# The last two pairs of chunks' up-projection as one block product with seven products for eight

## The chip, the cores and the metric

One core of one Trainium2 chip. The metric is the device time of one execution in microseconds (us); the time before is 1064.84 us, the median of 3 runs.

## The reference

Banded causal attention, then a feed-forward layer on its output, all in 32-bit floats:

```python
scores = scale * q @ k.T          # 8 batches, 8 heads, 576 positions, head size 64
scores += slopes[h] * -abs(rel)   # kept where 0 <= rel < 128, else -1e9
attn = exp(scores - max) / (sum + 1e-9)
x = (attn @ v)                    # to 4608 tokens x 512
h = x @ w_in                      # 512 -> 2048
g = h * sigmoid(1.702 * h)
out = g @ w_out                   # 2048 -> 512
```

## The kernel before

The feed-forward part takes 18 chunks of T = 256 tokens in 16 steps each, one step per block f of 128 hidden columns. So that products keep nearly full precision, each factor is split into a high and a low part and three products are made: high by high, high by low, low by high. In a step `Job.up` (L547 to L563) makes 12 matmuls of 256 columns into one of two banks h_ps (4 blocks of 128 of the model width, three products), ACT makes the tanh (L557), DVE finishes the gelu (L558), ACT rounds it to its high part gh (L561), POOL subtracts to get the low part gl (L562). `Job.down` (L565 to L573) makes 6 matmuls of 512 columns into acc0 and acc1. The loop emits the next step's up ahead of this step's down, so that the gelu of one step lies beside PE's work on others. At a chunk's end `finish` evacuates both accumulators by DVE and sends them out from ACT's queue; at its start `split_x` splits the chunk's x.

Attention runs beside it in ticks. A unit is a pair of heads and up to two query blocks; a tick moves several units one stage on each: load, split, scores (PE), bias and minimum (DVE), exponent (ACT), normalisation (DVE), transposes (PE), high and low part of the probabilities (ACT, DVE), mix (PE), sum into the chunk's x (`sum_up`, ACT, POOL, DVE). Batches 2 to 7 have 20 units each. A batch may start once the chunk named in `due` has begun, and must be done three steps ahead of the chunk that first needs it; the loop spreads its ticks evenly over the steps between. For batch 7 these are the start of chunk 13 and the start of chunk 15.

The weights come as 64-bit words in the first part and are decoded by ACT, DVE and POOL into w1[f] and w2[f], each with a high and a low part, 512 KB of room each, kept to the end.

The order on each engine is not that of the source alone: a scheduler with a timeline of its own places the instructions (the source order is its priority), except those that `keep_in_program_order` pins, the loads among them.

Of the kernel before, what the change touches and what calls it, by code (L numbers as in the profile page):

```python
# [142 lines left out]
def tile_kernel(ctx: ExitStack, tc: tile.TileContext, q0, k0, v0, qT, kT, v, w_in, w_out, out):  # L143
# [388 lines left out]
    def split_x(c, x):  # L532
        xh = xp.tile([P, NC, T], F32R, name="xh")
        xl = xp.tile([P, NC, T], F32R, name="xl")
        for k in range(NC):
            (nc.scalar.copy if c in BESIDE else nc.vector.tensor_copy)(xh[:, k], x[:, k])
# [1 line left out]
            sub.tensor_tensor(xl[:, k], x[:, k], xh[:, k].bitcast(F32), ALU.subtract)
        return xh, xl

    class Job:

# [4 lines left out]

        def up(self, f):
            h = ps.tile([P, T], F32, name="h_ps", bufs=2)
            ops = [(z, x, k) for z, x in ((0, self.xh), (1, self.xh), (0, self.xl)) for k in range(NC)]  # L550
            for n, (z, x, k) in enumerate(ops):
                nc.tensor.matmul(  # L552
                    h, w1[f][:, z, k * P:(k + 1) * P], x[:, k],
                    start=(n == 0), stop=(n == len(ops) - 1))
# [132 lines left out]
    begin(jobs[0])
    seen = 0
    flat = [(j, f) for j in jobs for f in range(j.f0, j.f1)]
    for now, (j, f) in enumerate(flat):  # L690
# [10 lines left out]
        pace, last = 0.0, 0  # L701
        for n, by, start in due:
            if start > seen:
                break
            last = n + 3
            pace = max(pace, (n + 3 - ticks - credit) / max(starts[by] - 1 - SLACK - now, 1))
        credit += pace
        while credit >= 1 and ticks < last:
            credit -= 1
            tick()  # L710
# [63 lines left out]
```

## Time and profile before

| | |
|---|---|
| time, median of 3 runs (lowest, highest) | 1064.84 us (1064.75, 1067.0) |
| the profiled execution: its time, its span | 1068.36 us, 1066.3 us |
| mean granted clock of TensorE | 0.995 |
| matmuls | 7041 |
| DMA | 78.45 MB, mean 74 GB/s |

In the page PE is TensorE's matmuls, PEld its weight loads, which overlap them, DVE VectorE, ACT ScalarE, POOL GpSimd, SP the engine from which the loads are issued. A name ending in q is an engine's sequencer or queue. A matmul's recorded duration includes its pipeline; the pace of a stream is read from the chain in order of time, where each piece counts once. A row of the chain has its start, its length, and what ran; a row of the timeline has start, length, engine, line, operation, and in brackets how long the engine had been idle and who released it. Rows of groups have the count, busy time, mean ns of one, and the idle time ahead of them.

### The profile page before, as it was taken

The numbers are of one execution on the slowest core, as the hardware profiler recorded it, in microseconds if no ns is written. First come the engines' busy times: TensorE is split into PE (matmuls) and PEld (weight loads), VectorE is DVE, ScalarE is ACT, GpSimd is POOL, SyncE is SP. The second block draws the span as 40 slices with busy tenths as digits, with TensorE's granted clock in tenths as the row PEclk, the third lists the DMA queues.
The fourth block names the chain that finished last, engine by engine and source line by source line (L and its number), as shares of the span: only waits on it lengthen the run. The fifth ranks groups of instructions, "written<-read, shape, count | busy, mean of one in ns | idle before, by whom it ended". The sixth has DMA issues, their size and how long they took to land.

```text
span 1066.3 us, 21362 instructions
## 1 busy us (share of the span) xinstructions
PE 1052.9 (99%) x7041; PEld 929.1 (87%) x7041; DVE 660.5 (62%) x2117; ACT 597.2 (56%) x1811; POOL 603.5 (57%) x863
## 2 busy tenths in 40 slices
PE   9899999999999999999999999999999999999998
PEld 5567787889989999999999999999999999998987
DVE  6797522568887777545767668767877687313121
ACT  6879853466666565535555556655665656322222
POOL 4579933567676666554656557656666665323232
PEclk9899999999999999999999999999999999999999
DMA  8872001223222132102121223212222221000000
GB/s 307 281 261 73 25 22 56 73 67 96 75 76 81 51 102 67 57 14 71 54 79 52 71 62 91 66 60 78 79 63 85 57 78 28 20 2 20 1 21 20
DMA packets 88109, 78.45 MB, mean 74 GB/s; under 512 B 36800, under 2 KB 79296, under 8 KB 88000
## 3 DMA queue, kind: packets, MB, share of 16 engines
q1 hardware_dynamic: 82240, 67.14, 21.4%
q10 hardware_dynamic: 5760, 9.96, 2.6%
q8 instruction: 55, 0.90, 0.3%
q14 instruction: 54, 0.44, 0.1%
HBM read 67.63 MB, written 9.44 MB: 72 GB/s over the span
## 4 chain that ended last, share of the span: by engine, by line
PE 94%; DVE 3%; ACT 1%; DMA 1%; issue 1%; POOL 0%; SPq 0%; DVEq 0%; POOLq 0%; ACTq 0%
PE h_ps L552 38%; PE acc L571 37%; PE s_ps L334 5%; PE x_ps L499 5%; PE t_ps L442 4%; PE x_ps L476 2%; PE t_ps L419 1%; PE sb_ps L324 1%; PE s_ps L324 1%; DVE wc L213 1%; DMA rw<-w_out 1%; ACT pb L374 1%; DVE rec L392 0%; PE acc L189 0%; DVE rw L212 0%
## 5 line engine op out<-in xcount | busy, mean ns | idle before, releaser
L562 POOL TENSOR_TENSOR gl<-g,gh 128x256 fp32r<-128x256 f32 x288 | 218.0, 757 | 292.2 <-ACT gh L561 224.9
L552 PE MATMUL h_ps<-xh,w 128*128 128x256 f32 x2304 | 370.2, 284 | 1.1 <-POOL w L217 0.6
L552 PEld LDWEIGHTS h_ps<-xh,w 128*128 128x128 f32 x2304 | 328.5, 189 | 34.5 <-issue 2.8
L571 PE MATMUL acc<-w,gh 128*128 128x512 f32 x1152 | 324.9, 400 | 0.0
L558 DVE SCALAR_TENSOR_TENSOR g<-g,h_ps 128x256 f32<-128x256 f32 x288 | 119.6, 415 | 207.9 <-ACT g L557 206.5
L557 ACT ACTIVATE g<-h_ps 128x256 f32<-128x256 f32 x288 | 110.4, 383 | 229.4 <-PE h_ps L552 207.3
L571 PEld LDWEIGHTS acc<-w,gh 128*128 128x128 f32 x1152 | 196.5, 189 | 27.9 <-ACT g L557 0.3
L552 PE MATMUL h_ps<-xl,w 128*128 128x256 f32 x1152 | 194.6, 280 | 0.0
L561 ACT CAST gh<-g 128x256 fp32r<-128x256 f32 x288 | 116.9, 406 | 129.5 <-DVE g L558 121.1
L571 PE MATMUL acc<-w,gl 128*128 128x512 f32 x576 | 188.0, 401 | 0.0
L552 PEld LDWEIGHTS h_ps<-xl,w 128*128 128x128 f32 x1152 | 164.2, 188 | 6.0
L312 POOL TENSOR_TENSOR K<-rk,K 128x384 fp32r<-128x384 f32 (+1 forms) x120 | 109.0, 909 | 65.2 <-ACT Q L292 15.9
L381 ACT ACTIVATE pb<-pb,mins 128x256 f32<-128x256 f32 (+2 forms) x216 | 104.9, 487 | 43.8 <-DVE mins L362 40.1
L571 PEld LDWEIGHTS acc<-w,gl 128*128 128x128 f32 x576 | 92.6, 188 | 9.5 <-issue 0.9
L311 POOL TENSOR_TENSOR Q<-rq,Q 64x256 fp32r<-64x256 f32 (+1 forms) x120 | 83.1, 692 | 22.2 <-DVE K L310 4.9
L406 DVE TENSOR_SCALAR pb<-pb,rec 128x256 f32<-128x256 f32 (+2 forms) x216 | 91.8, 461 | 3.2
L362 DVE CUSTOM_DVE_ANT_0 pb<-s_ps,bias 128x256 f32<-128x256 f32 (+3 forms) x240 | 85.7, 377 | 4.1 <-PE s_ps L334 2.8
L392 DVE TENSOR_SCALAR rec<-sums 128x2 f32<-128x2 f32 (+3 forms) x144 | 48.5, 336 | 58.4 <-ACT pb L381 53.6
L334 PE MATMUL s_ps<-K,Q 128*128 128x256 f32 (+1 forms) x432 | 79.8, 289 | 0.4 <-DVE mins L362 0.4
L310 DVE CAST K<-rk 128x384 fp32r<-128x384 f32 (+1 forms) x120 | 52.5, 438 | 41.2 <-PE s_ps L334 34.2
L461 DVE TENSOR_TENSOR pl<-t_ps,ph 128x512 fp32r<-128x512 f32 (+2 forms) x120 | 72.2, 604 | 9.3 <-ACT ph L455 6.6
L442 PE MATMUL t_ps<-ident,pb 128*128 128x128 f32 x408 | 74.2, 272 | 0.0
(68 smaller groups left out, 1322.2 us busy)
## 6 DMA issues: line engine op xcount, KB each, us to landing
rk<-kT SPq DMA_DIRECT2D x72, 192.0 KB, 2.5
rq<-qT SPq DMA_DIRECT2D x96, 128.0 KB, 2.3
out<-o ACTq DMA_DIRECT2D x36, 256.0 KB, 2.1
rw<-w_in SPq DMA_DIRECT2D x16, 512.0 KB, 6.5
rw<-w_out SPq DMA_DIRECT2D x16, 512.0 KB, 7.0
rk<-kT SPq DMA_DIRECT2D x48, 128.0 KB, 2.2
rv<-v SPq DMA_DIRECT2D x96, 64.0 KB, 1.9
rq<-q SPq DMA_DIRECT2D x16, 128.0 KB, 2.6
```

Source lines behind the costliest of these rows:

```text
L312: nc.gpsimd.tensor_tensor(K2, rk, K1.bitcast(F32), ALU.subtract)
L334: nc.tensor.matmul(u.s[:b.rows, e, b.first:b.end], u.Q[:, b.q0 - u.q0:b.q0 - u.q0 + b.rows], k[:, ko:ko + b.end - b.first], start=(z == 0) ...
L362: nc.vector.tensor_tensor_reduce(b.p[ra:rb, cs:b.end], u.s[ra:rb, e, cs:b.end], bias[head][ra:rb, cs:b.end], -SCALE, BIG, ALU.add, ALU.min ...
L381: nc.scalar.activation(live, live, AF.Exp, bias=u.mins[:b.rows, e:e + 1], scale=-1.0, accum_out=u.sums[:b.rows, e:e + 1],)
L406: nc.vector.tensor_scalar(live, live, u.rec[:rows, e:e + 1], None, ALU.mult)
L442: nc.tensor.transpose(u.t[:c.n, w:w + b.rows], b.p[:b.rows, col:col + c.n], ident[:b.rows, :b.rows])
L552: nc.tensor.matmul(h, w1[f][:, z, k * P:(k + 1) * P], x[:, k], start=(n == 0), stop=(n == len(ops) - 1))
L557: nc.scalar.activation(g, h, AF.Tanh, scale=0.851)
L558: nc.vector.scalar_tensor_tensor(g, g, 1.0, h, ALU.add, ALU.mult)
L561: nc.scalar.copy(gh, g)
L562: nc.gpsimd.tensor_tensor(gl, g, gh.bitcast(F32), ALU.subtract)
L571: nc.tensor.matmul(acc, g[:, t * P:(t + 1) * P], w2[f][:, z], start=(f == self.f0 and n == 0), stop=(f == self.f1 - 1 and n == 2))
```

## The change

The up-projection of chunks 14 to 17 is done for two chunks at a time. The block product is of two by two blocks: two hidden blocks f = 2j, 2j + 1, the two halves of the model width, and the two chunks. In Strassen's way (Winograd's form) seven products of sums of blocks replace the eight plain ones; each is still three products of high and low parts. The sums of x (T1 to T4) are made at a pair's start in `Pair.split`, into the room of w1[0] to w1[6]. The sums of weights (S1 to S4) are made eight times in `sums(j)`, one about every 24 steps from step 33 on, and are written with the plain blocks A11, A12 and A22 to DRAM, 56 parts of 256 KB. In the pairs, 512 KB tiles with two parts each are read back for each product in turn, into a ring of five in the room of w1[7] to w1[11], and once more for the second pair. Two banks X and Y gather the products; `up(j, q)` makes them in quarters, with parts of the sums added in SBUF by ACT and DVE. Four accumulators take the down-projection, those of h_ps among them. `split_x` has its tiles in halves. Batch 7 is due at the start of the pair, that is of chunk 14.

```diff
+S0 = 14
+RING = 5
+SUMS_FROM = 33
+ORDER = "A11", "A12", "S2", "S3", "S1", "S4", "A22"
+OPERANDS = "B11", "B21", "T2", "T3", "T1", "B22", "T4"
...
+    def sums(j):
+        f, g = w1[2 * j], w1[2 * j + 1]
+        H = 2 * P
+        for name, src in (("A11", f[:, :, :H]), ("A12", f[:, :, H:]), ("A22", g[:, :, H:])):
+            nc.sync.dma_start(part(j, name), src.bitcast(F32))
+        a = ffn.tile([P, 2 * H], F32, name="sa", tag="o", bufs=3)
+        b = ffn.tile([P, 2 * H], F32, name="sb", tag="o", bufs=3)
+        nc.gpsimd.tensor_tensor(a, g[:, 0].bitcast(F32), g[:, 1].bitcast(F32), ALU.add)
+        nc.gpsimd.tensor_tensor(b, f[:, 0].bitcast(F32), f[:, 1].bitcast(F32), ALU.add)
...
+        for s, names in ((a, ("S3", "S1")), (b, ("S2", "S4"))):
+            st = xp.tile([P, 2, 2 * H], F32R, name="st", tag="x0")
+            nc.scalar.copy(st[:, 0], s)
+            nc.gpsimd.tensor_tensor(st[:, 1], s, st[:, 0].bitcast(F32), ALU.subtract)
+            for i, name in enumerate(names):
+                nc.sync.dma_start(part(j, name), st[:, :, i * H:(i + 1) * H].bitcast(F32))
+    def factor(n):
+        tile_, side = divmod(n, 2)
+        while len(ring) < min(tile_ + RING, (NCH - S0) // 2 * len(parts)):
+            r = const.tile([P, 2, 2, 2 * P], F32R, name="ring", tag=f"w1_{len(OPERANDS) + len(ring) % RING}")
+            nc.sync.dma_start(r.bitcast(F32), parts[len(ring) % len(parts)])
+            ring.append(r)
+        return ring[tile_][:, side]
...
+            cut("B11", a1)
+            cut("B21", a2)
+            nc.vector.tensor_tensor(a1, b1, a1, ALU.subtract)
+            cut("B22", b2)
+            nc.vector.tensor_tensor(b1, b2, b1, ALU.subtract)
+            nc.vector.tensor_tensor(b2, b2, a1, ALU.subtract)
+            cut("T2", b2)
+            cut("T3", b1)
+            cut("T1", a1)
+            nc.vector.tensor_tensor(a2, a2, b2, ALU.subtract)
+            cut("T4", a2)
...
+        def up(self, j, q):
+            if q == 0:
+                self.X = ps.tile([P, T], F32, name="X_ps", tag="t_ps", bufs=2)
+                self.product(j, 0, self.X, True)
...
+                nc.scalar.copy(self.p, self.X)
+                self.Y = ps.tile([P, T], F32, name="Y_ps", tag="t_ps", bufs=2)
+                self.product(j, 1, self.Y, True)
+                nc.vector.tensor_tensor(self.p, self.Y, self.p, ALU.add)
...
+                self.gelu(self.g[:, :T], self.p)
+            elif q == 1:
+                self.product(j, 2, self.X, False)
...
+                nc.scalar.copy(self.u[:, :T], self.X)
+            elif q == 2:
+                self.product(j, 3, self.Y, True)
+                self.product(j, 4, self.X, False)
+                nc.scalar.copy(self.u[:, T:], self.X)
+                nc.vector.tensor_tensor(self.u[:, T:], self.Y, self.u[:, T:], ALU.add)
+            else:
+                self.product(j, 5, self.X, False)
+                self.gelu(self.g[:, T:], self.X)
+                self.keep(2 * j, self.g)
+                self.product(j, 6, self.Y, False)
+                nc.vector.tensor_tensor(self.u[:, :T], self.Y, self.u[:, :T], ALU.add)
...
+                self.gelu(g, self.u)
+                self.keep(2 * j + 1, g)
...
+    for c in range(S0, NCH):
+        starts[c] = steps + (c - S0) // 2 * 2 * NF
...
+        pair = Pair(c)
+        pair.split()
+        seen = c + 1
+        for i in range(NF // 2 * 4):
+            now += 1
+            advance(now)
+            pair.up(i // 4, i % 4)
+            if before is None:
+                if i == 1:
+                    j.down(f)
+                    j.finish()
+                if i >= 4:
+                    pair.down(i // 4 - 1, i % 4)
+            elif i < 4:
+                before.down(NF // 2 - 1, i)
+            else:
+                pair.down(i // 4 - 1, i % 4)
```

PE in a middle step of chunk 17 before, and, below it, in one block of the second pair now. h_ps and acc are the banks of up and down; X_ps, Y_ps and accs are theirs in the pair; xh, xl, xT and xB are parts of x, ring holds the products' weights, gs both parts of the gelu.

```order
L552 MATMUL h_ps<-xh,w_14_1616 128x256 x8
L552 MATMUL h_ps<-xl,w_14_1616 128x256 x3
L571 MATMUL acc_15076<-w_12_1466,gh 128x512
L571 MATMUL acc_15077<-w_12_1466,gh 128x512
L552 MATMUL h_ps<-xl,w_14_1616 128x256
L571 MATMUL acc_15076<-w_12_1466,gl 128x512
L571 MATMUL acc_15077<-w_12_1466,gl 128x512
L552 MATMUL h_ps<-xh,w_15_1682 128x256 x8
```

```order
L679 MATMUL Y_ps<-xT_14759,ring 128x256 x6
L732 MATMUL accs<-w_11_1383,gs 128x512 x11
L679 MATMUL X_ps<-xT_14762,ring 128x256 x6
L732 MATMUL accs<-w_11_1383,gs 128x512
L679 MATMUL X_ps<-xB_14751,ring 128x256 x6
L679 MATMUL Y_ps<-xT_14766,ring 128x256 x6
L679 MATMUL X_ps<-xB_14744,ring 128x256 x6
L679 MATMUL Y_ps<-xB_14747,ring 128x256 x6
L732 MATMUL accs<-w_12_1500,gs 128x512 x8
L679 MATMUL X_ps<-xT_14756,ring 128x256 x6
L732 MATMUL accs<-w_12_1500,gs 128x512 x4
```

Where down matmuls of one step stood between parts of the next step's up, the down work of a block now stands together: one down matmul lies between T1 (xT_14762) and B22 (xB_14751), none between B22, T4 (xT_14766) and the next B11 (xB_14744). Of these rows B22 has a wait on ACT, T4 and the next B11 on DVE.

The end of attention on PE, before (in the last steps ahead of chunk 15) and now (at the end of chunk 13); s_ps holds scores, t_ps transposes, x_ps the mix.

```order
L552 MATMUL h_ps<-xl,w_13_1499 128x256 x4
L499 MATMUL x_ps<-ph,VV 128x256
L499 MATMUL x_ps<-pl,VV 128x256
L499 MATMUL x_ps<-ph,VV 128x256
L499 MATMUL x_ps<-pl,VV 128x256
L499 MATMUL x_ps<-ph,VV 128x128
L499 MATMUL x_ps<-pl,VV 128x128
L552 MATMUL h_ps<-xh,w_14_1616 128x256 x5
L571 MATMUL acc_13439<-w_12_1466,gh 128x512
```

```order
L583 MATMUL acc_12732<-w_15_1802,gl 128x512
L583 MATMUL acc_12733<-w_15_1802,gl 128x512
L449 MATMUL t_ps<-ident,pb 128x128 x7
...
L507 MATMUL x_ps<-pl,VV 128x256
L679 MATMUL X_ps<-xB_13944,ring 128x256 x6
L449 MATMUL t_ps<-ident,pb 128x128 x2
...
L507 MATMUL x_ps<-pl,VV 128x128
L679 MATMUL Y_ps<-xB_13947,ring 128x256 x6
L679 MATMUL Y_ps<-xT_13959,ring 128x256 x6
L679 MATMUL X_ps<-xT_13956,ring 128x256 x6
```

The last transposes and mixes stood between matmuls of the feed-forward steps; now they follow the last of these, with two products of the pair among them.

SP's queue early in the program now, where the weights (rw) are loaded between those of attention:

```order
L162 DMA rw_4_350<-w_out 128x512 [waits DMAHW5_49]
L162 DMA VV<-v 128x3x128 [waits DMAHW6_49]
L616 DMA part_84<-w_0_417 128x2x256 [waits DMAHW7_49,Pool_49]
L616 DMA part_84<-w_0_417 128x2x256 [waits DMAHW0_49]
L162 DMA rq<-q 128x64 [waits DMAHW1_49,PE_49]
L162 DMA rk<-k 128x192 [waits DMAHW2_49]
L162 DMA rw_5_409<-w_in 128x512 [waits DMAHW3_49]
```

The two stores of plain weight blocks (L616) are new there; of the 24 such stores eight stand between the loads of weights.

More of the change, by code (lines that the diff above doesn't have):

```diff
@@ L433, in flip @@
             return
-        u.t = ps.tile([P, 4 * P], F32, name="t_ps", bufs=2)
+        u.t = ps.tile([P, 4 * P], F32, name="t_ps", tag="s_ps" if paired else "t_ps", bufs=1 if paired else 2)
         u.ph = att.tile([P, 4 * P], F32R, name="ph")
@@ L532, in split_x @@
     def split_x(c, x):
[L533 to L534 removed]
+        xh, xl = [], []
         for k in range(NC):
[L536 removed]
+            if k % 2 == 0:
+                h = xp.tile([P, 2, T], F32R, name="xh", tag=f"xh{k // 2}")
+                l = xp.tile([P, 2, T], F32R, name="xl", tag=f"xl{k // 2}")
+            xh.append(h[:, k % 2])
+            xl.append(l[:, k % 2])
+            (nc.scalar.copy if c in BESIDE else nc.vector.tensor_copy)(xh[k], x[:, k])
             sub = nc.vector if k % 2 else nc.gpsimd
[L538 removed]
+            sub.tensor_tensor(xl[k], x[:, k], xh[k].bitcast(F32), ALU.subtract)
         return xh, xl
@@ L671, in tile_kernel @@
     jobs.append(Job(0, F0, NF, jobs[0]))
-    jobs += [Job(c, 0, NF) for c in range(2, NCH)]
+    jobs += [Job(c, 0, NF) for c in range(2, S0)]
     starts = {}
@@ L685, in begin, with advance @@
         j.up(j.f0)
+    def advance(now):
+        nonlocal credit
+        pace, last = 0.0, 0
+        for n, by, start in due:
+            if start > seen:
+                break
+            last = n + 3
+            pace = max(pace, (n + 3 - ticks - credit) / max(starts[by] - 1 - SLACK - now, 1))
+        credit += pace
+        while credit >= 1 and ticks < last:
+            credit -= 1
+            tick()
     begin(jobs[0])
-    seen = 0
+    seen, made = 0, 0
     flat = [(j, f) for j in jobs for f in range(j.f0, j.f1)]
@@ L699, in tile_kernel @@
                 decode_next()
[L701 to L710, printed above, removed]
+        advance(now)
+        if now >= SUMS_FROM and made < NF // 2 and (now - SUMS_FROM) * NF // 2 >= made * (len(flat) - SUMS_FROM):
+            sums(made)
+            made += 1
         if now + 1 < len(flat):
@@ L717, in tile_kernel @@
                 seen = max(seen, nj.c)
-        j.down(f)
-        if f == j.f1 - 1:
-            j.finish()
+            j.down(f)
+            if f == j.f1 - 1:
+                j.finish()
+    while made < NF // 2:
+        sums(made)
+        made += 1
+    paired = True
+    before = None
+    for c in range(S0, NCH, 2):
+        pair = Pair(c)
[3 more added lines that the diff above has]
+            now += 1
+            advance(now)
+            pair.up(i // 4, i % 4)
+            if before is None:
+                if i == 1:
+                    j.down(f)
+                    j.finish()
+                if i >= 4:
+                    pair.down(i // 4 - 1, i % 4)
+            elif i < 4:
+                before.down(NF // 2 - 1, i)
+            else:
+                pair.down(i // 4 - 1, i % 4)
+        before = pair
+    for q in range(4):
+        before.down(NF // 2 - 1, q)
 def build(nc, arrays):
```

71 lines of the change are left out of this document (70 added, 1 removed).

## The prediction

> **What bounds the kernel now.** I read the page first: busy shares, the span in slices, and the chain that ended last.
>
> ```profile
> span 1066.3 us, 21362 instructions
> PE 1052.9 (99%) x7041; PEld 929.1 (87%) x7041; DVE 660.5 (62%) x2117; ACT 597.2 (56%) x1811; POOL 603.5 (57%) x863
> ...
> PE   9899999999999999999999999999999999999998
> ...
> DVE  6797522568887777545767668767877687313121
> ACT  6879853466666565535555556655665656322222
> POOL 4579933567676666554656557656666665323232
> ...
> PE 94%; DVE 3%; ACT 1%; DMA 1%; issue 1%; POOL 0%; SPq 0%; DVEq 0%; POOLq 0%; ACTq 0%
> PE h_ps L552 38%; PE acc L571 37%; PE s_ps L334 5%; PE x_ps L499 5%; PE t_ps L442 4%; PE x_ps L476 2%; PE t_ps L419 1%; PE sb_ps L324 1%; PE s_ps L324 1%; DVE wc L213 1%; DMA rw<-w_out 1%; ACT pb L374 1%; DVE rec L392 0%; PE acc L189 0%; DVE rw L212 0%
> ```
>
> PE is the bound: 94% of the chain, and from the second slice in tens to the end it never rests. So a matmul less is time won, and an idle moment of PE is time lost, one for one. The other engines have their idle time in the last six slices; before those DVE runs at 6 to 8 tenths.
>
> Next the chain in order of time, for what a matmul costs in a dense stream and for where attention ends:
>
> ```profile
> 908.38 0.44 PE t_ps L442 x4
> 918.25 0.64 PE x_ps L499 x6
> 1000.24 1.40 PE h_ps L552 x12
> 1001.65 1.40 PE acc L571 x6
> ```
>
> Twelve 256-column matmuls take 1.40 us, 0.117 each; six of 512 columns take as long, 0.234 each; a transpose takes 0.11. A step (up 12, down 6) is 2.80 us. The last attention matmul is at 918.9, and 143 us, 51 steps, follow: attention is over three steps ahead of chunk 15, while chunk 14 still gives PE work to do beside it.
>
> The timeline near the end gives the handovers, and one place early on shows PE being released by ACT:
>
> ```profile
> 36.87 0.35 ACT L485 COPY xf<-x_ps 128x256 f32<-128x256 f32 x1
> 37.12 0.58 ACT L427 COPY pw<-t_ps 128x512 f32<-128x512 f32 x1
> 37.75 0.18 PEld L324 LDWEIGHTS sb_ps<-rk,rq 64*128 64x128 f32 x1 [1.33 <-ACT pw L427]
> ...
> 1052.87 0.63 PE L552 MATMUL h_ps<-xl,w 128*128 128x256 f32 x4
> 1053.34 1.10 PE L552 MATMUL h_ps<-xh,w 128*128 128x256 f32 x8
> 1053.59 0.39 ACT L557 ACTIVATE g<-h_ps 128x256 f32<-128x256 f32 x1 [1.52 <-PE h_ps L552]
> 1054.01 0.42 DVE L558 SCALAR_TENSOR_TENSOR g<-g,h_ps 128x256 f32<-128x256 f32 x1 [2.38 <-ACT g L557]
> ```
>
> From the start of PE's next matmul (1053.34) to ACT's start (1053.59) pass 0.25 us; ACT to DVE 0.03; ACT's end at 37.70 to PE's restart 0.05. The weight load, too, started only after ACT's release.
>
> **The change, part by part.**
>
> *Products.* Chunks 14 to 17 had 4 x 16 x 12 = 768 up matmuls; two pairs x 8 blocks x 7 products x 6 matmuls are 672, of the same 256 columns. The down matmuls stay 384. So 96 x 0.117 = **-11.2 us**. That is all that can be won there, bar the tail: the last four evacuations are staggered and shared by two engines, where two stood behind each other (1.29 us at 1061.71 for both, below). One fewer at the end: **-0.6**.
>
> ```profile
> 1061.71 1.29 DVE L587 TENSOR_SCALAR o<-acc 128x512 f32<-128x512 f32 x2 [3.06 <-PE acc L571]
> ```
>
> *Waits on the two banks X and Y.* In the new order PE runs per block: T3 into Y, eleven down matmuls, T1 into X, one down matmul, B22 into X, T4 into Y, then the next block's B11 into X. B22 adds onto X, so it waits until ACT has copied X after T1. From T1's end: 0.25 + 0.35 (the copy) + 0.05 = 0.65; the one down matmul covers 0.234; 0.42 is left. B11 starts X anew, so it waits for tanh and for DVE's product, both of which read X after B22: 0.25 + 0.39 + 0.03 + 0.42 + 0.05 = 1.14, of which T4 covers 0.70; 0.44 is left. The other waits of a block are covered: the eleven down matmuls are 2.6 us over a copy; the high part of gs is ready at 1.14 - 0.05 + 0.63, its low part 1.44 later (rows below), and PE reaches them after T4, the wait, and two products (2.5 us), and eight down matmuls more. Each wait also holds the weight load, so a matmul's own 0.117 may come on top: between 0.43 and 0.55, I take 0.5. There are 16 waits of the first kind and 15 of the second: 31 x 0.5 = **+15.5** (13.3 to 17).
>
> ```profile
> L217 POOL TENSOR_TENSOR w<-wc,w 128x512 fp32r<-128x512 f32 x32 | 45.9, 1442 | 6.6 <-ACT w L216 6.4
> L216 ACT CAST w<-wc 128x512 fp32r<-128x512 f32 x32 | 20.2, 630 | 4.8 <-DVE wc L213 4.6
> L213 DVE SCALAR_TENSOR_TENSOR wc<-wc,rw 128x512 int32<-128x512 int32 x32 | 32.4, 1017 | 9.5 <-ACT wc L211 9.4
> ```
>
> *Attention squeezed into chunk 13.* A pair needs both its chunks, so batch 7 is now due at the start of chunk 14, not 15: its ticks fall into 13 steps, not 29. From chunk 13's split to the pair's third product the order gives DVE 233 instructions, and PE 314 matmuls of 256 columns, 102 of 512 and 71 of 128: 36.7 + 23.9 + 7.8 = 68.4 us of PE. DVE's cost per instruction comes from the middle of the kernel, where the mix is the same:
>
> ```profile
> 300.00:880.00 580.00, 579.51 (x3976) 533.03 (x3975) 410.25 (x1359) 330.22 (x1012) 356.03 (x547) 1.00 0.24 68
> 26.00:52.00 26.00, 23.14 (x136) 15.40 (x136) 18.24 (x59) 21.10 (x63) 13.38 (x13) 0.87 0.80 279
> 52.00:78.00 26.00, 23.52 (x153) 17.16 (x151) 24.01 (x48) 20.28 (x63) 19.73 (x18) 0.93 0.82 281
> ```
>
> The columns after the stretch are PE, PEld, DVE, ACT, POOL busy, then clock, DMA share and GB/s. 410.25 / 1359 = 0.302 us; 233 x 0.302 = 70.4, plus 0.7 for each of five 512-wide operations with both inputs in SBUF (1.02 by L213): 74 us. DVE becomes the bound of that stretch. Never resting, it costs 74 - 68.4 = 5.6 us; at the best share that any stretch shows, 24.01 of 26, 80.4 - 68.4 = 12; with durations shorter than their mean, nothing. The order agrees: after chunk 13's last down matmul PE has only transposes, attention products and two new products, each behind DVE. I take **+9** (0 to 20).
>
> *The first block of pair 14* has no down work beside it, and its sums depend on the last attention columns. After T3's low part come DVE's subtraction (1.0), ACT's cast (0.63), POOL's low part (1.44); PE has 1.2 us to do meanwhile, so 2.0 idle. T1 and B22 each sit 0.65 behind a copy, and B11 0.44: 3.7 in all, 0.9 of which is counted above: **+3** (1 to 5). At the change of pairs B22 lacks its down matmul (0.23), and two evacuations of 0.58 by ACT and two DMA issues stand ahead of the copy it waits for: **+1.5** (0 to 4).
>
> *Weight sums and the queues.*
>
> ```profile
> out<-o ACTq DMA_DIRECT2D x36, 256.0 KB, 2.1
> rw<-w_in SPq DMA_DIRECT2D x16, 512.0 KB, 6.5
> rw<-w_out SPq DMA_DIRECT2D x16, 512.0 KB, 7.0
> ...
> 26.45 7.62 DMA rw<-w_out
> ```
>
> Eight times two casts of 0.63 on ACT, two adds and two low parts of 1.44 on POOL, and four adds on DVE are spread over 190 steps in which those engines have over a quarter of their time free. But st has one buffer: ACT's second cast waits for POOL's low part and two 256 KB stores of the first (1.44 + 2.1 + issue, some 4 us), and the gelus queue behind it on ACT, the next loads behind the stores on SP. ACT has five to twelve other instructions in between; I take 0.25 us of PE per sum, **+2** (0 to 8). The 24 stores of plain weight blocks are queued as soon as a block is decoded, eight of them between the weight loads. That is 2.1 MB, 7.5 us at 281 GB/s, in a stretch where DMA engines are busy 0.80 and the chain waits 7.62 us for one weight load; two stores precede that load's successors. **+1** (0 to 5).
>
> The ring brings 56 tiles of 512 KB, 29.4 MB in about 185 us, 160 GB/s, where 281 was moved. A slot is refilled four tiles, about 11 us, ahead; such a load landed in 6.5 to 7.0 us when all queues were full. I cost it at nothing; were that cover gone, each block would wait for its tiles.
>
> Sum: -11.2 - 0.6 + 15.5 + 9 + 3 + 1.5 + 2 + 1 = **+20.2**: a span of 1086.5. The profiled execution took 1068.36, 2.06 more than its span and 3.5 more than the median; on the median of 1064.84 the forecast is **1085 us**. All low ends together give 1067, all high ends 1112; they will not all meet.
>
> **Rivals.**
>
> *The products win (chance 0.12).* ACT and DVE are nearly idle in the last slices, so the bank waits could be shorter than these handovers say, and attention could drain beside chunk 13. The turning point is 11.8 us of added idle time. With half of the bank waits (7.7) and no squeeze it is 1061; with none at all 1053. Against it: the copy between T1 and B22 is a single chain with one matmul over it, and operations of that shape take 0.35 and 0.39 in the rows.
>
> *The drain slows PE's clock and DVE falls short (0.10).* In 26 to 52 us PE was busy 23.14 of 26 us and its clock 0.87. If the 35 us around the end of chunk 13 run so, 4.5 us are added; with DVE at 0.81 of the stretch (18.24 + 24.01 of 52) 74 / 0.81 - 68.4 = 23 instead of 9: 1085 + 4.5 + 14 = 1103. By the Trainium skill ("TensorE: Matmul & The Clock Gate", Part 1) the clock halves only after an idle window of about 3.4 us; by that rule waits of half a microsecond would leave it alone, only the drain could trip it, and the sum would stay at 1085. The trace agrees in part: at 0.87 PE's longest listed wait was 1.6 us.
>
> ```profile
> PE acc L189 <- POOL ident masks.py:199: 1.6, 1, 1.6
> ```
>
> *No change (0.05).* Bank waits at 12, no squeeze, nothing else: 1065 to 1067.
>
> **How the numbers follow.** The forecast's own case, 1068 to 1102, has 0.70; the faster rival 0.12, no change 0.05, over 1102 0.10, and 0.03 is for slower cases just under it. From 1060 to 1102 leaves out most of the faster rival and the slow one, two in ten. A measurement of this kernel can tell about 0.2%, 2.1 us, from no change. Faster 0.12, same 0.05, slower 0.83.
>
> **What would show it.** Right: in the last 180 us PE idles some 0.5 us ahead of B22 (released by ACT's copy) and of each next B11 (by DVE), a block taking 11.5 us instead of the dense 42 x 0.117 + 24 x 0.234 = 10.5; DVE at nine tenths through chunk 13 and PE idle for several us between chunk 13's last down matmul and T2. Wrong: a block at 10.6 us, PE at 9 tenths across chunk 13, PE waiting for ring tiles, or a start that is later by more than 5 us.

## The result, and the profile after

The changed kernel takes 1108.45 us (median of 4 runs, 1108.4 to 1110.16) against 1064.8 of the kernel before: 1.0409 times as long, 95% interval 1.0391 to 1.0427. That is 43.6 us more, where 20.2 were forecast; the profiled execution took 1108.4 with a span of 1106.3.

The page of the changed kernel: span, busy time, slices, and the chain that ended last.

```profile
span 1106.3 us, 21523 instructions
PE 1065.8 (96%) x6945; PEld 927.8 (84%) x6945; DVE 733.0 (66%) x2167; ACT 618.0 (56%) x1845; POOL 648.0 (59%) x863
...
PE   9899999999989998999999999999999988999997
...
DVE  6877522288887888544868787866788984345332
...
PE 75%; DVE 10%; ACT 3%; issue 3%; POOL 2%; DMA 2%; SPq 0%; ACTq 0%; POOLq 0%; DVEq 0%
```

The 96 matmuls are gone, as counted (6945 for 7041). But PE has fallen from 94% to 75% of the chain, DVE has risen from 3% to 10%, and the slices in which PE rests are not only the last ones: two with an 8 stand at 304 to 332 and 415 to 443 us, where no pair is near. A third such place, near 712 us, does not show in a slice; it shows in the stretches below.

To date the loss, the start of a chunk is taken as its first up matmul. For chunk 13, before (first fence) and after (second), in the timeline:

```profile
814.26 0.71 PE L571 MATMUL acc<-w,gl 128*128 128x512 f32 x2
814.81 0.63 PE L552 MATMUL h_ps<-xh,w 128*128 128x256 f32 x4
```

```profile
835.12 0.28 PE L507 MATMUL x_ps<-pl,VV 128*128 128x256 f32 x1
835.24 0.28 PE L564 MATMUL h_ps<-xh,w 128*128 128x256 f32 x1
```

In the same way chunk 1 starts at 89.2 before and 85.6 after, and the last matmul ends at 1061.9 and 1101.0. So the stretches are:

| | before | after | difference | forecast |
|---|---|---|---|---|
| up to chunk 1 | 89.2 | 85.6 | -3.6 | |
| chunk 1 to chunk 13 (weight sums, plain stores) | 725.6 | 749.6 | +24.0 | +3 |
| chunk 13 to the last matmul (squeeze, pairs) | 247.1 | 265.8 | +18.7 | +17.8 |
| last matmul to the end of the span | 4.4 | 5.3 | +0.9 | -0.6 |

The first row is the profiled execution of before alone, which lay 3.5 us over its median. The pairs, about which the prediction argued at length, came out at the sum that it gave; the weight sums and stores, which it costed at 3 us, cost 24.

The stretches by chunk after show where the 24 lie (columns as in the prediction; chunks 4, 6, 7 and 11):

```profile
306.00:372.00 66.00, 63.69 (x417) 57.73 (x418) 52.27 (x176) 39.26 (x122) 46.09 (x71) 0.95 0.33 93
...
431.00:485.00 54.00, 50.97 (x334) 45.60 (x333) 29.86 (x95) 23.63 (x70) 30.32 (x42) 1.00 0.21 62
485.00:538.00 53.00, 53.00 (x361) 48.67 (x360) 28.77 (x88) 25.84 (x75) 25.23 (x40) 1.00 0.21 58
...
712.00:775.00 63.00, 59.80 (x391) 54.20 (x391) 43.37 (x141) 33.22 (x101) 39.11 (x58) 0.97 0.28 80
```

Chunks 4, 6 and 11 begin 5 to 7 us after a sum's first add (299.1, 426.2 and 707.0); no sum stands ahead of chunk 7, and there PE is busy 53.00 of 53. In chunks 4 and 11 the granted clock falls as well. The timeline at the start of chunk 4, cut to DVE, POOL and those who wait:

```profile
303.61 0.41 DVE L623 TENSOR_TENSOR sb<-sa,sb 128x256 f32<-128x256 f32 x1
...
304.55 0.63 DVE L624 TENSOR_TENSOR sb<-sb 128x256 f32<-128x256 f32 x1
304.86 0.91 POOL L574 TENSOR_TENSOR gl<-g,gh 128x256 fp32r<-128x256 f32 x1
305.10 2.28 DVE L548 CAST xh<-xf 128x256 fp32r<-128x256 f32 x3
305.73 1.31 POOL L628 TENSOR_TENSOR st<-sa,st 128x512 fp32r<-128x512 f32 x1
305.97 0.38 PE L564 MATMUL h_ps<-xh,w 128*128 128x256 f32 x1 [0.91 <-DVE xh L548]
...
307.24 0.39 PE L564 MATMUL h_ps<-xh,w 128*128 128x256 f32 x1 [0.89 <-DVE xh L548]
...
308.44 0.40 ACT L388 ACTIVATE pb<-pb,mins 128x128 f32<-128x128 f32 x1 [3.71 <-DVE mins L369]
...
308.80 1.22 PE L341 MATMUL s_ps<-K,Q 128*128 128x256 f32 x4 [0.30 <-DVE mins L369]
```

DVE never rests here. The sum's last adds stand ahead of the casts that make chunk 4's xh; three casts take 2.28 us, and PE, the scores and ACT's exponents wait behind them. Over the whole trace such a cast takes 0.29 us where POOL does nothing and 0.82 where POOL works beside it for at least 95% of it (medians of 6 and 16).

The clock in finer stretches: first the 3.4 us ahead of two of its falls, then chunk 4's start, then 724 us and the start of the first pair.

```profile
304.29:307.70 3.41, 1.62 (x8) 0.98 (x6) 3.41 (x6) 0.43 (x2) 3.33 (x4) 1.00 0.00 0
...
720.80:724.20 3.40, 1.29 (x9) 0.98 (x9) 3.37 (x11) 2.69 (x8) 1.30 (x3) 0.99 0.42 154
```

```profile
306.00:312.00 6.00, 4.72 (x15) 3.48 (x16) 5.97 (x16) 2.55 (x8) 5.71 (x9) 0.64 0.27 89
312.00:318.00 6.00, 4.97 (x28) 4.39 (x28) 5.00 (x22) 3.50 (x11) 3.64 (x5) 0.79 0.26 81
```

```profile
724.00:730.00 6.00, 6.00 (x36) 5.72 (x35) 3.49 (x13) 3.41 (x11) 3.88 (x5) 0.72 0.21 70
...
901.00:912.00 11.00, 8.03 (x38) 6.33 (x38) 8.43 (x33) 6.89 (x20) 2.18 (x5) 0.84 0.14 49
912.00:924.00 12.00, 9.12 (x55) 8.07 (x56) 7.66 (x16) 6.06 (x13) 4.36 (x4) 0.86 0.39 128
```

In the first two rows PE is busy less than half of 3.4 us, and right behind them its clock is halved: the granted clock is 0.50 from 307.8 to 314.5 and from 724.2 to 727.5. (0.36 + 0.21) x 6 = 3.4 us are lost at chunk 4 and 0.28 x 6 = 1.7 at 724, together 5.1 of the 24; and 0.16 x 11 + 0.14 x 12 = 3.4 where attention drains before the first pair.

Last, the two bank waits in a block of pair 14, as the prediction described them (T1, one down matmul, ACT's copy, B22; then tanh, DVE's product, the next B11):

```profile
976.55 0.88 PE L679 MATMUL X_ps<-xT,ring 128*128 128x256 f32 x6
977.26 0.39 PE L732 MATMUL accs<-w,gs 128*128 128x512 f32 x1
977.47 0.37 ACT L711 COPY u<-X_ps 128x256 f32<-128x256 f32 x1 [4.43 <-PE X_ps L679]
...
977.89 0.98 PE L679 MATMUL X_ps<-xB,ring 128*128 128x256 f32 x6 [0.23 <-ACT u L711]
978.71 0.88 PE L679 MATMUL Y_ps<-xT,ring 128*128 128x256 f32 x6
...
979.32 0.42 DVE L685 SCALAR_TENSOR_TENSOR g<-g,X_ps 128x256 f32<-128x256 f32 x1 [1.03 <-ACT g L684]
...
979.80 0.98 PE L679 MATMUL X_ps<-xB,ring 128*128 128x256 f32 x6 [0.21 <-DVE g L685]
```

The first matmul of B22 starts 0.63 us after the down matmul ahead of it, which takes 0.234. From B11 to B11 a block takes 11.48 us, twelve times out of fifteen to 0.01; 11.5 were forecast. The gaps beyond the dense pace sum to 8.2 us ahead of and in the sixteen B22 and 7.9 in the B11.

### The profile page after: what moved, and what is told of

It is laid out like the page before. It is cut to its first block, busy times and chain, and to the rows that moved or that the text cites. A ratio compares the mean times of both kernels' runs of the same rounds, so it can differ in the third digit from the quotient of the medians.

```text
span 1106.3 us, 21523 instructions
## 1 busy us (share of the span) xinstructions
PE 1065.8 (96%) x6945; PEld 927.8 (84%) x6945; DVE 733.0 (66%) x2167; ACT 618.0 (56%) x1845; POOL 648.0 (59%) x863
## 4 chain that ended last, share of the span: by engine, by line
PE 75%; DVE 10%; ACT 3%; issue 3%; POOL 2%; DMA 2%; SPq 0%; ACTq 0%; POOLq 0%; DVEq 0%
PE acc L583 23%; PE h_ps L564 23%; PE accs L732 8%; PE X_ps L679 5%; PE s_ps L341 4%; PE x_ps L507 4%; PE t_ps L449 3%; PE Y_ps L679 2%; PE x_ps L484 1%; DVE xf L537 1%; DVE pb L413 1%; DVE rec L399 1%; DVE xh L548 1%; DVE pb L369 1%; DVE K L317 1%
## 5 line engine op out<-in xcount | busy, mean ns | idle before, releaser
L564 PE MATMUL h_ps<-xh,w 128*128 128x256 f32 x1792 | 291.8, 287 | 6.0 <-DVE xh L548 3.0
L564 PEld LDWEIGHTS h_ps<-xh,w 128*128 128x128 f32 x1792 | 255.3, 190 | 31.5 <-DVE g L570 4.6
L574 POOL TENSOR_TENSOR gl<-g,gh 128x256 fp32r<-128x256 f32 x224 | 172.0, 769 | 151.5 <-ACT gh L573 114.1
L583 PE MATMUL acc<-w,gh 128*128 128x512 f32 x896 | 258.8, 404 | 0.8 <-ACT gh L573 0.7
L583 PEld LDWEIGHTS acc<-w,gh 128*128 128x128 f32 x896 | 154.6, 190 | 24.8 <-ACT gh L573 1.8
L564 PE MATMUL h_ps<-xl,w 128*128 128x256 f32 x896 | 155.1, 283 | 0.2
L583 PE MATMUL acc<-w,gl 128*128 128x512 f32 x448 | 148.3, 405 | 2.0 <-POOL gl L574 2.0
L690 POOL TENSOR_TENSOR gs<-g,gs 128x512 fp32r<-128x512 f32 x32 | 42.2, 1320 | 126.2 <-PE Y_ps L679 83.8
L732 PE MATMUL accs<-w,gs 128*128 128x512 f32 x384 | 98.0, 392 | 0.9 <-ACT gs L689 0.9
L318 POOL TENSOR_TENSOR Q<-rq,Q 64x256 fp32r<-64x256 f32 (+1 forms) x120 | 84.2, 702 | 22.2 <-DVE pb L413 3.2
L732 PEld LDWEIGHTS accs<-w,gs 128*128 128x128 f32 x384 | 69.1, 189 | 12.6 <-ACT gs L689 1.1
```

The lines of the kernel that those rows point to most:

```text
L564: nc.tensor.matmul(h, w1[f][:, z, k * P:(k + 1) * P], x[k], start=(n == 0), stop=(n == len(ops) - 1))
L574: nc.gpsimd.tensor_tensor(gl, g, gh.bitcast(F32), ALU.subtract)
L583: nc.tensor.matmul(acc, g[:, t * P:(t + 1) * P], w2[f][:, z], start=(f == self.f0 and n == 0), stop=(f == self.f1 - 1 and n == 2))
L732: nc.tensor.matmul(self.acc[t], g[:, y, t * P:(t + 1) * P], w2[f][:, z], start=(f == 0 and n == 0), stop=(f == NF - 1 and n == 2))
```

## The experiments

Three theories of the 24 us stood from the start. Theory 1: the sums' work on POOL and DVE stands ahead of attention and of the next chunk's split. Rivals: the stores on SP's queue (2), and ACT's cast waiting for the one buffer st, the risk that the prediction had named (3). All times are medians; the kernel before was timed beside each group at 1064.2 to 1065.6. "Idle" of PE means that its matmuls' starts lie further apart than 0.117, 0.234 or 0.11 us by their kind, a lowered clock included.

### The halves of the change apart

**plain_stores.** `sums` stores plain halves for S1 to S4:

```diff
-        a = ffn.tile([P, 2 * H], F32, name="sa", tag="o", bufs=3)
...
+        for name, src in (("S1", g[:, :, :H]), ("S2", g[:, :, H:]), ("S3", f[:, :, :H]), ("S4", f[:, :, H:])):
+            nc.sync.dma_start(part(j, name), src.bitcast(F32))
```

> Leaves out the sums' arithmetic: the same 56 stores of 256 KB go out at the same places in the code, but S1 to S4 are plain halves of the weights, so chunks 14 to 17 compute something else in the same time. The two traces show PE idle 24.1 us in chunks 2 to 12 (189 to 775 us) after the change, 2.0 before. Theory 1, the sums' work on POOL and DVE stands ahead of attention and of the next chunk's split: without it 1108.5 - 20 = about 1088 us. Rival 2, the stores on SP's queue hold up attention's loads: no change, 1106 to 1109. Rival 3, ACT's second cast waits for the one buffer st: about 1088 as well, since the casts go too.

Measured 1089.97 us, 1.023 (1.0212 to 1.0248). Chunk 13 starts at 814.9. The arithmetic is worth 18.5 us, and the stores themselves are out as its cause. One part of rival 2 is left: with the arithmetic went also what SP's queue waited for, 150.0 us in all, for the low parts in st. adds_only and casts_only below settle that.

**sums_mid_chunk.** The steps, and a tie of the first add to POOL's low part of that step, so that the scheduler keeps the place:

```diff
-SUMS_FROM = 33
+SUMS_AT = 98, 102, 106, 114, 118, 122, 146, 150
...
+        in_turn([after, nc.gpsimd.tensor_tensor(a, g[:, 0].bitcast(F32), g[:, 1].bitcast(F32), ALU.add)])
```

> Same work, other steps: the eight sums are held at steps 2, 6 and 10 of chunks 6 and 7 and steps 2 and 6 of chunk 9, where DVE is busy 30 of 54 us, none within the last five steps of a chunk. As they stand, four begin 0.6 to 6.9 us ahead of a chunk's start (306, 432, 539, 712 us) and the four chunks that follow hold 19.5 us of PE's idle time; the other four sums have about 4 in all. Theory 1 (what counts is what the sum is put ahead of): 15 to 20 us faster, 1089 to 1093. Rival 3 (the wait for st is the same wherever the sum stands): within 4 us of 1108. Rival 2 (the same stores): within 4 us of 1108.

Measured 1093.21 us, 1.0268 (1.0243 to 1.0293): 15.2 of the 18.5 us come back by place, with the same work.

**sums_alone** has no pairs; it also leaves out the last chunk's last step of down matmuls and its output. **sums_alone_whole** has that step. Of both, the line that takes chunks 14 to 17 out of pairs:

```diff
-    jobs += [Job(c, 0, NF) for c in range(2, S0)]
+    jobs += [Job(c, 0, NF) for c in range(2, NCH)]
```

> The sums, their stores and the split in halves at the same steps as in the changed kernel, but chunks 14 to 17 go on unpaired, as in the kernel before; what the sums store is read by nothing. Theory 1 (two separate losses, one per half of the change): the sums' 20 us without the pairs' 20, so 1064.8 + 20 = 1083 to 1088. Rival 2 (the loss up to chunk 13 comes from the scheduler's other order for the pairs, not from the sums): 1065 to 1070.

> The run named sums_alone left out the last chunk's last step of down matmuls and its output; this one has them. By its starts of chunks the sums cost 23 us up to chunk 13 (838.0 against 814.8) and 25.5 up to chunk 14. Theory 1: with the last step and its output, 1064.5 + 24 to 27 = 1088 to 1092. Rival 2 (the scheduler's order for the pairs): already out by that run's starts; it would need 1065 to 1070.

Measured 1088.02 us, 1.0206 (1.0182 to 1.023), and, whole, 1091.68, 1.024 (1.0218 to 1.0261). The sums lose their time with no pair in the program: 22.2 us over stores_alone below, which differs only by their arithmetic.

**pairs_in_order.** PE's matmuls of the pairs, from the second block on, tied to the order of the code:

```diff
+                line.append(nc.tensor.matmul(
...
+    in_turn(line[7 * 6:])
```

> From the second block of pair 14 on PE's matmuls are tied to the order of the code, in which six down matmuls (1.40 us) stand between T1 and B22 and six more between T4 and the next B11. After the change PE idles 8.2 us ahead of the sixteen B22 and 7.9 ahead of the sixteen B11. Theory 1 (31 bank waits of 0.5 us with too few matmuls over them): a block falls from 11.48 to 10.5 us, 1108.5 - 15 = about 1093. Rival 2 (the next wait is right behind, for the low part of gs or for the ring's load): a block stays at 11 or more, 1100 to 1108.

Measured 1093.62 us, 1.027 (1.0245 to 1.0294): 14.8 us less than the changed kernel. The gaps at B22 and B11 sum to 2.1 us instead of 16.1. In its timeline six down matmuls now cover ACT's copy, and no wait stands at B22:

```profile
1024.27 0.88 PE L680 MATMUL X_ps<-xT,ring 128*128 128x256 f32 x6
1024.99 1.55 PE L733 MATMUL accs<-w,gs 128*128 128x512 f32 x6
1025.19 0.37 ACT L712 COPY u<-X_ps 128x256 f32<-128x256 f32 x1 [2.39 <-PE X_ps L680]
...
1026.38 0.88 PE L680 MATMUL X_ps<-xB,ring 128*128 128x256 f32 x6
```

A block takes 10.56 us, near the dense 10.5; the waits were the scheduler's order, not the algorithm's.

### What in a sum costs

Eight edits of `sums`, at the same places in the code but for DVE's part in adds_in_two_steps. The scheduler places the adds anew in each. Where there are adds, the first of them still begins from 7 us ahead to 2 us after the starts of chunks 6, 8 and 11; at chunk 4 it begins 7 to 17 us ahead. The first two edits split a sum. **adds_only** ends `sums` after the adds and stores plain halves as above; **casts_only** has no adds:

```diff
+        a, b = f[:, 0].bitcast(F32), g[:, 0].bitcast(F32)
```

> Of the sums only the six adds (two on POOL, four on DVE) are left; S1 to S4 are stored as plain halves of the weights, with no cast on ACT, no low part on POOL and no buffer st. All the sums' arithmetic together was worth 18.5 us (1108.5 to 1090.0), and it starts chunk 13 at 835.2 or at 814.9 us. Theory 1 (the adds, on POOL and in DVE's queue just ahead of a chunk's start, delay attention and the split): most of it stays, chunk 13 starts at 828 to 835, 1102 to 1108. Rival 3 (the cast waiting for the one buffer st, with the gelus behind it): chunk 13 starts at 815 to 820, 1090 to 1094.

> The other half: no adds; ACT casts the first half of each weight pair into st, POOL makes its low part, and both are stored, with the same one buffer st. Chunks 14 to 17 compute something else in the same time. Theory 1: chunk 13 starts at 815 to 822, 1090 to 1096. Rival 3 (the one buffer): at 828 to 835, 1102 to 1108.

**adds_on_pool** keeps the whole computation and moves DVE's four adds to POOL; one of the four is shown:

```diff
-        nc.vector.tensor_tensor(a[:, H:], a[:, :H], a[:, H:], ALU.add)
+        nc.gpsimd.tensor_tensor(a[:, H:], a[:, :H], a[:, H:], ALU.add)
```

> The sums' four adds on DVE go to POOL, which then has six; DVE has none. Within theory 1 two readings: if the place in DVE's queue is what counts (each sum's adds take 2.8 us there, 22.6 in all), the loss falls by about half, chunk 13 at 823 to 828, 1096 to 1101; if it is POOL's long operations (1.3 us each, during which DVE's two-input and copy operations also stretch: the split's cast 0.46 before and 0.51 after on the mean, up to 1.35), it stays or grows, chunk 13 at 833 to 842, 1106 to 1115.

**pool_adds_only** and **dve_adds_only** cut adds_only in two; DVE's adds then read the weights:

```diff
-        nc.gpsimd.tensor_tensor(a, g[:, 0].bitcast(F32), g[:, 1].bitcast(F32), ALU.add)
...
-        nc.vector.tensor_tensor(a[:, H:], a[:, :H], a[:, H:], ALU.add)
+        nc.vector.tensor_tensor(a[:, H:], ga[:, 0, :H], ga[:, 0, H:], ALU.add)
```

> Of each sum only POOL's two 512-wide adds are left (nothing reads them), at the same places; S1 to S4 are stored as plain halves, so chunks 14 to 17 compute something else in the same time. No arithmetic is 1090.0, all six adds 1110.9. Theory 1a (each engine's share by itself: POOL's six adds cost 8.5 us, two of these are 2.7 of 5.9 us of POOL): 1093 to 1096. Theory 1b (POOL's 1.3 us operations are the cause, whatever DVE does): 1100 or more.

> Of each sum only DVE's four adds of 256 columns are left; they read the weights themselves, so they wait for nothing on POOL. Theory 1a (each share by itself): 1110.9 - 5 = 1104 to 1108. Theory 1c (DVE's adds cost most when they stand behind POOL's, in the queue ahead of attention and the split, or run beside them: 1.50 us for one that takes 0.41 alone): alone they cost 4 x 0.42 = 1.7 us of DVE a sum, 1092 to 1099. Theory 1b: about 1090.

**adds_unlinked** has both, POOL writing to sa and DVE to sb:

```diff
-        nc.gpsimd.tensor_tensor(b, f[:, 0].bitcast(F32), f[:, 1].bitcast(F32), ALU.add)
+        nc.gpsimd.tensor_tensor(a, f[:, 0].bitcast(F32), f[:, 1].bitcast(F32), ALU.add)
...
+        nc.vector.tensor_tensor(b[:, H:], ga[:, 0, :H], ga[:, 0, H:], ALU.add)
```

> Both sets of adds at the places that they have in adds_only, but DVE's read the weights and no longer POOL's result, and what they make is used by nothing; S1 to S4 are stored as plain halves, so chunks 14 to 17 compute something else in the same time. Theory 1d (the tie: DVE's queue, with attention, the gelus and the next split in it, waits for POOL's 1.3 us adds): the two parts by themselves, 1090 + 0.6 + 3.3 = 1094, up to 1097. Rival 1e (running beside each other is enough): 1106 to 1111.

**adds_on_dve** and **adds_in_two_steps** keep the whole computation too; in the second `after` is DVE's product of the gelu two steps later. One line of the first, then two of the second:

```diff
-        nc.gpsimd.tensor_tensor(a, g[:, 0].bitcast(F32), g[:, 1].bitcast(F32), ALU.add)
+        nc.vector.tensor_tensor(a, g[:, 0].bitcast(F32), g[:, 1].bitcast(F32), ALU.add)
```

```diff
+            held[now + 2] = made, *adds(made)
...
+        in_turn([after, nc.vector.tensor_tensor(a[:, H:], a[:, :H], a[:, H:], ALU.add)])
```

> The whole computation, with POOL's two adds of 512 columns moved to DVE: six adds there, 1.0 + 1.0 + 4 x 0.42 = 3.7 us of DVE a sum where it had 2.8, none on POOL. Theory 1d: the tie is gone, so 1093 to 1100 although DVE does more. Rival 1e (DVE's time is what counts): slower than the changed kernel, 1108 to 1115. Rival 1f (the buffers): between, since they are held about as long.

> The whole computation; POOL's adds where they were, DVE's four adds tied to DVE's product of the gelu two steps of the code later, which by the order puts them in the middle of chunks, up to fourteen steps behind POOL's. The tie is kept, but POOL has long ended; sa and sb are held all that time. Theory 1d: 1092 to 1098. Rival 1f (sa and sb hold two of the three buffers that attention's copies use): 1108 or more.

The last two columns are worked out from each trace, in us: from the start of chunk 1 to that of chunk 13, and the time in it in which DVE is busy.

| run | time | ratio (95%) | chunk 1 to 13 | DVE busy |
|---|---|---|---|---|
| plain_stores (no arithmetic) | 1089.97 | 1.0230 (1.0212, 1.0248) | 729.9 | 488.8 |
| casts_only | 1090.49 | 1.0236 (1.0218, 1.0254) | 730.4 | 491.2 |
| pool_adds_only | 1090.61 | 1.0244 (1.0228, 1.0260) | 730.3 | 491.5 |
| dve_adds_only | 1093.32 | 1.0278 (1.0261, 1.0294) | 731.5 | 507.1 |
| adds_in_two_steps | 1094.67 | 1.0283 (1.0267, 1.0299) | 734.2 | 513.8 |
| adds_on_pool | 1098.94 | 1.0319 (1.0301, 1.0337) | 740.7 | 507.2 |
| adds_unlinked | 1102.44 | 1.0356 (1.0332, 1.0380) | 744.6 | 519.6 |
| adds_on_dve | 1106.16 | 1.0391 (1.0370, 1.0412) | 745.2 | 526.8 |
| changed kernel | 1108.45 | 1.0409 (1.0391, 1.0427) | 749.6 | 519.4 |
| adds_only | 1110.92 | 1.0439 (1.0406, 1.0472) | 750.3 | 516.1 |

Rivals 2 and 3 fall here. adds_only has no st, and no wait of SP for it, and the whole loss stays (21.0 us over plain_stores); casts_only has st, its stores and 122.7 us of SP waiting for them, and costs nothing that can be measured. Rival 1f falls with adds_in_two_steps, where sa and sb are held longest and most of the loss is gone. What is left are the six adds, and they are not the sum of their parts: POOL's two cost 0.6 us, DVE's four 3.4, both together 21.0. Two stretches of the timeline show what happens. The same place ahead of chunk 6, in adds_only and then in dve_adds_only, from the same instruction on:

```profile
425.71 1.30 POOL L619 TENSOR_TENSOR sa<-w 128x512 f32<-128x512 f32 x1
425.78 0.41 DVE L468 TENSOR_TENSOR pl<-t_ps,ph 128x256 fp32r<-128x256 f32 x1
...
426.97 1.29 POOL L620 TENSOR_TENSOR sb<-w 128x512 f32<-128x512 f32 x1
427.04 1.49 DVE L621 TENSOR_TENSOR sa<-sa 128x256 f32<-128x256 f32 x1 [0.85 <-POOL sa L619]
...
428.46 0.41 DVE L570 SCALAR_TENSOR_TENSOR g<-g,h_ps 128x256 f32<-128x256 f32 x1
...
429.72 1.44 DVE L548 CAST xh<-xf 128x256 fp32r<-128x256 f32 x2
...
431.84 0.49 DVE L548 CAST xh<-xf 128x256 fp32r<-128x256 f32 x2
```

```profile
422.05 0.41 DVE L468 TENSOR_TENSOR pl<-t_ps,ph 128x256 fp32r<-128x256 f32 x1
...
422.38 0.41 DVE L620 TENSOR_TENSOR sa<-w 128x256 f32<-128x256 f32 x1
...
425.02 0.41 DVE L570 SCALAR_TENSOR_TENSOR g<-g,h_ps 128x256 f32<-128x256 f32 x1
...
425.35 0.90 DVE L548 CAST xh<-xf 128x256 fp32r<-128x256 f32 x4
```

With POOL's adds DVE first waits 0.85 us in its queue for the first of them; then its add of 0.41 us is stretched to 1.49 by the second. From pl's start to the end of the fourth xh pass 6.55 us instead of 4.20, and chunk 6 has 5.7 us of idle PE instead of none. Both effects count: without the tie (adds_unlinked) 12.5 us of loss over plain_stores remain, with it 21.0; without POOL's adds 3.4.

DVE's time in the table does not give the loss by itself. 18 us more of it than in plain_stores cost 1.6 us between chunks 1 and 13 in dve_adds_only, but 11 in adds_on_pool; 27 to 38 us cost 15 to 20, the most in adds_only, where they are fewest; with DVE's adds mostly in the middle of chunks (adds_in_two_steps) 25 us cost 4. The place is shown to matter most. That a sum costs what it takes of DVE's time beyond the little that DVE has to spare ahead of a chunk's start fits the rows above, but no run shows it apart from the rest; the lowered clock comes on top.

Several forecasts missed. adds_only came out above the range of theory 1, pool_adds_only below 1a and 1b, and adds_unlinked and adds_on_dve between 1d and 1e, so neither the tie alone nor DVE's load beside POOL alone is the cause. In range were casts_only (theory 1), dve_adds_only (1c), adds_on_pool (the place in DVE's queue) and adds_in_two_steps (1d). How much of the 20 is tie, stretch and the scheduler's order after the adds, which changes a little with each edit, stays open.

The Trainium skill ("SBUF — State Buffer", "Who interferes with whom") says that a DVE instruction with two inputs in SBUF contends with a POOL instruction that reads SBUF, that a copy or cast in one of DVE's two-port modes and a POOL instruction block each other for a whole instruction, and that a DVE instruction with at most one input in SBUF outside those modes does not contend with POOL. The traces agree, though no row names a cast's mode: the cast goes from 0.29 to 0.82 us, an add with both inputs in SBUF from 0.41 to 1.49 (the two fences above), but the chunks' gelu product, with one input in PSUM, takes 0.42 alone and 0.41 beside POOL.

### The rest of chunk 1 to 13

Without any arithmetic that stretch is still 4.3 us longer than before (729.9 and 725.6).

**split_halves_alone** is the kernel before with xh and xl as halves; **stores_alone** has the 56 plain stores as well. The halves:

```diff
-        xh = xp.tile([P, NC, T], F32R, name="xh")
+                h = xp.tile([P, 2, T], F32R, name="xh", tag=f"xh{k // 2}")
```

> The kernel before with one edit of the change: the split tiles xh and xl in halves; no sums, no stores, no pairs. If the halves cost the 4 us: 1067 to 1069. If the stores do: 1064 to 1066. If it is the scheduler's different order, anything between 1062 and 1068.

> The halves and all 56 stores of plain weight blocks, no arithmetic, no pairs. If the stores cost the 4 us: 1067 to 1070, with the lengthening in chunk 1, where the plain blocks go out between the weight loads. If nothing does: 1064 to 1066.

Measured 1067.56 us, 1.0032 (1.0019 to 1.0045), and 1069.47, 1.0045 (1.0033 to 1.0058). The halves, which the prediction did not cost at all, take some 3 us; why they do was not tried. The stores take perhaps 2, but the two intervals overlap. Chunk 1 lasts 68.3 us with the halves and 74.3 with the stores, half of which chunk 2 gives back.

### Put together again

**one_pair_plain** (`S0 = 16`, tied order, plain stores), **one_pair_sums_apart** (the same with the sums at steps 98, 106, 114, 122, adds on POOL, and 238, 242, 246, 250), **two_pairs_sums_apart** (both pairs, tied order, adds on POOL, the steps of sums_mid_chunk).

```diff
-S0 = 14
+S0 = 16
+SUMS_AT = 98, 106, 114, 122, 238, 242, 246, 250
```

> Only chunks 16 and 17 are a pair, so batch 7 is due at chunk 15 again, as in the kernel before; the order of the matmuls is tied as in pairs_in_order; the sums' arithmetic is left out (plain halves stored), so chunks 16 and 17 compute something else in the same time. With two pairs, no arithmetic and the tied order it should be 1090.0 - 14.9 = 1075, of which the stretch of chunk 13 to the pair's first products holds some 12 us of idle PE. Theory 1 (that stretch is attention squeezed from 29 steps into 13): with one pair it goes, and what is left is 1064.8 - 48 x 0.117 - 0.6 + 1 to 4 for the first block = 1060 to 1063. Rival (it is the change from single chunks to a pair, whichever chunk it stands at): 1066 to 1072.

> One pair, tied order, and the whole computation: four sums in the middle of chunks 6 and 7 with their adds on POOL, four from the last steps of chunk 14 on, where attention has ended, with the last four adds on DVE. Theory 1 (a sum is free where DVE and POOL have nothing due): as with plain stores and 0 to 3 more, 1060 to 1065, against 1064.8 before. Rival (a sum costs its 2 to 3 us wherever it stands): 1076 or more.

> Both pairs, tied order, adds on POOL, the eight sums in the middle of chunks 6, 7 and 9. Theory 1, the pieces add up: 1093.6 of pairs_in_order less 15 to 18 for the sums = 1075 to 1079, the rest over 1064.8 being the squeeze of chunk 13 and the first blocks. Rival (the sums' cost moves to another chunk): 1085 or more.

Measured 1064.81 us, 1.0005 (0.9994 to 1.0016); 1076.09, 1.011 (1.0091 to 1.013); 1081.32, 1.016 (1.0146 to 1.0175).

With one pair the stretch from chunk 13 to the last matmul has 3 us of idle PE instead of 18 in pairs_in_order: the squeeze goes, as theory 1 said, and the change from chunks to a pair costs 3 us at most at this place. The time, 1064.81, lies between the forecasts of theory 1 (1060 to 1063) and of the rival (1066 to 1072), and is that of before: one pair saves what the halves and the stores cost, even with sums for nothing. two_pairs_sums_apart, too, came out between its forecasts (1075 to 1079, and 1085 or more): the pieces add up but for some 2 us. No version here beats the kernel before.

one_pair_sums_apart went against theory 1 and for its rival. The four sums around chunk 15, where DVE is busy three tenths, cost some 10 us of idle PE; the four in chunks 6 and 7 cost 2. Its timeline at the start of chunk 15 shows the same things at work:

```profile
923.08 1.78 DVE L548 CAST xh<-xf 128x256 fp32r<-128x256 f32 x2 [0.56 <-PE h_ps L564]
...
923.37 1.34 POOL L619 TENSOR_TENSOR sa<-w 128x512 f32<-128x512 f32 x1
...
924.67 1.34 POOL L620 TENSOR_TENSOR sb<-w 128x512 f32<-128x512 f32 x1
924.78 2.38 DVE L550 TENSOR_TENSOR xl<-xf,xh 128x256 fp32r<-128x256 f32 x2
...
927.54 1.21 PE L564 MATMUL h_ps<-xh,w 128*128 128x256 f32 x8 [1.22 <-DVE g L570]
...
940.35 1.28 DVE L599 TENSOR_SCALAR o<-acc 128x512 f32<-128x512 f32 x2
...
941.18 0.71 PE L583 MATMUL acc<-w,gh 128*128 128x512 f32 x2 [2.13 <-DVE o L599]
```

An engine with seven tenths of its time free was no protection here, where the few instructions that PE waits for fall beside POOL's adds; that these adds do it is read from the rows and not shown apart. Chunk 14's output o, whose buffer st shares, also comes late there; that it waits for st is read from the code and not shown.

## Why the prediction was wrong

- *Products, -11.2*: held; 96 matmuls fewer, and the dense pace in both kernels. The tail's -0.6 did not: +0.9. ACT now issues four last stores where it issued two, two of them behind its own evacuations, and the last is issued 1.9 us after the last matmul's end where it was 1.5.
- *Bank waits, +15.5*: held in mechanism and size. Idle at B22 and B11 16.1 us, a block 11.48 for 11.5, and 14.8 us back when the order covers them (14.0 of them by the gaps in the two traces).
- *Squeeze +9, first block +3, change of pairs +1.5*: together 13.5, and by the trace 18.7 + 11.2 - 16.1 = 13.8, of which 3.4 are the lowered clock. That was priced in the rival "the drain slows PE's clock" at 4.5; it came true without DVE falling as short as that rival had it. So the agreement of the sum is in part luck: without the clock the three terms come to 10.4. The mechanism was the one forecast: from chunk 13's first up matmul to the pair's third product (835.24 to 915.66) 80.4 us pass with 68.4 us of dense matmuls in them, DVE is busy 71.3 of them, and PE idles 5.8 us between chunk 13's last down matmul and that product. In the working behind this term 74 at 24.01 of 26 is 80.1, not 80.4, and the cited wait of 1.6 us stands in the program's first microseconds; from 26 to 52 us the longest is 1.5. Neither changes a bound or a chance. The change of pairs cost nothing: the two blocks beside it take 22.94 us together, and two others 22.96.
- *Ring at nothing*: held. No wait of PE after 912 us names the ring, and its tiles landed 3.1 to 4.8 us after they were issued.
- *Weight sums, +2 (0 to 8)*: this is the step that failed. "Those engines have over a quarter of their time free" and "0.25 us of PE per sum" average over 190 steps. Four of the eight sums were placed by the scheduler just ahead of a chunk's start, where DVE has no quarter free: in the kernel before it is busy 0.95, 0.84, 0.90 and 0.84 of the ten us around the starts of these chunks (309.8, 427.1, 531.4 and 700.0). Each of the four cost 3 to 6 us of PE. The risk named in that paragraph, st's single buffer, was worth nothing; the one that mattered, POOL's and DVE's adds beside and behind each other, was not looked for, though the trace of before already had the split's cast at two lengths, 0.29 us without POOL at work and 0.82 beside it. The term measured 18.5 us, so even the top of its range, 8, was too low.
- *Startup stores, +1*: near (about 2). The split in halves had no term; it cost 3.

By medians: halves and stores 5.0 (1069.47 - 1064.48), pairs with their squeeze 20.5 (1089.97 - 1069.47), sums' arithmetic 18.5 (1108.45 - 1089.97); 44.0 in all, 43.6 measured.

## What to carry to other kernels

Small work "in the idle quarter" of an engine is priced at the places where it lands, not by the mean: look at what the scheduler puts it ahead of, and at the slack of that engine there. Of the 18.5 us here, another place gave back 15.2, and 13.8 came back where DVE's part stood some steps behind POOL's, mostly in the middle of chunks. Giving the adds to one engine gave back 9.5 (POOL) or only 2.3 (DVE), so it is no cure by itself. And before a wait is charged to an algorithm, try whether tying the order removes it.

## What the runs showed of the hardware

The clock of PE was halved without PE ever being idle for long. In the changed kernel 3.41 us with PE busy 1.62 (304.29 to 307.70) and 3.40 us with 1.29 (720.80 to 724.20), the longest single wait 1.75 us, were each followed by a granted clock of 0.50, for 6.8 and 3.4 us. The Trainium skill ("TensorE: Matmul & The Clock Gate", Part 1) lets the clock fall after an idle window of about 3.4 us; the length fits, but here a window less than half busy was enough, and the measurement decides. The records of all twenty traces together give the share: the clock changes only on a grid of 3.41 us, and after the first 65 us PE's matmuls, counted at their dense pace (0.117, 0.234 and 0.11 us), fill at most 0.41 of each of the 47 pieces of that grid that end in a fall, and at least 0.39 of each of the some 5800 at full clock that do not.

What a DVE instruction costs beside POOL depends on its form, and for the cast also on who began first. In the kernel before, 19 casts of the split have POOL at work beside at least 95% of them. Seven of these began within 0.01 us of the start of POOL's operation and took 0.28 or 0.29 us, as alone. The other twelve began 0.10 to 0.44 us after it, took 0.73 to 0.83, and each ended 0.15 us after POOL's operation did. So the length of POOL's operation sets the price of a cast that comes second.
